# A static slot schedule for the backward pass of one-query attention, with the o sums taken over columns of E as weights

## The chip, the cores and the metric

The kernel runs on one core of a Trainium2 chip. The metric is the device time of one execution in microseconds. Each execution is classed as fast or slow, and only fast ones are compared.

The engines are called as the profile calls them. PSUM is the memory that PE's results go to in these kernels. Recorded texts and some headings say bank for the storage of one PSUM tile; the traces name tiles, and no run here shows banks. PE is TensorE's matmuls, PEld its weight loads. ACT is ScalarE, DVE is VectorE, POOL is GpSimd and SP issues the loads. PEclk is the granted TensorE clock: 1.0 is full speed.

## The reference

For 64 independent heads there is one query q, 8192 keys K and values V of 128 elements in bf16, and the gradient d of the output. The kernel returns the output o and the gradients dq, dK and dV.

```python
scores = einsum("bhqd,bhkd->bhqk", q, k) * scale      # Sq = 1, Sk = 8192, D = 128
p = softmax(scores)
o = einsum("bhqk,bhkd->bhqd", p, v)                   # and its vjp for grad_out
```

Per head this means s = K q, dp = V d, E = exp(scale (s - max)), the sums l = sum E and delta, then dS = E (dp - delta), dq = dS K, o = E V, and the outer products dK = dS q and dV = p d. K and V are read once and dK and dV written once: 8.39 MB per head, 537 MB in all.

## The kernel before

K and V come in with the keys on the partitions, so each 128x128 block is transposed on PE before it serves as weights for s and dp. A head has 8 chunks of 16 blocks, four of K and four of V.

```python
for w, src in enumerate((kt, vt)):
    for c in range(NCH):                                   # 4 chunks each
        tp = ps_tp.tile([P, CH, P], BF16, tag="tp")
        for i in range(CH):                                # 16 transposes, 128 columns moving
            nc.tensor.transpose(tp[:, i, :], src[:, c * CH + i, :], ident_bf[:])
        ev = evp.tile([P, CH, P], BF16, tag="ev")
        nc.scalar.copy(out=ev[:], in_=tp[:])               # eviction on ACT: out of PSUM
        for i in range(CH):                                # 16 score products, one column moving
            nc.tensor.matmul(sdp[:, w, n : n + 1], lhsT=ev[:, i, :], rhs=qdT[:, w, bh : bh + 1], ...)
# ... then the softmax chain: maximum (DVE, PE, DVE, PE, DVE), E_f (ACT), sums (PE), dS (DVE)
for w, (src, col, norm) in enumerate(((kt, dS_bf, rls), (vt, E_bf, rl))):
    for n in range(NT):                                    # 64 dq products, then 64 o products
        nc.tensor.matmul(acc[:, w : w + 1], lhsT=src[:, n, :], rhs=col[:, n : n + 1], ...)
# ... then 8 outer products of 1.22 us on DVE, and two stores
```

One PSUM tile per head, sdpw, holds s, dp, the transposed maximum, its broadcast and the two sums. The build orders the instructions by its own scheduler.

## Time and profile before

| | before |
|---|---|
| time, median of 9 runs | 1401.55 us (1393.88 to 1408.60) |
| PE, ACT, DVE busy | 88%, 71%, 53% |
| mean granted clock | 0.716 |
| first to last maximum of a head, 63 heads | 1342.7 us, 21.3 us per head |

The first view is the page of the kernel before: the busy times, two rows of the 40 slices (tenths of full clock, tenths of DMA time), and the chain of work that ended last, by engine.

```profile
PE 1228.4 (88%) x24964; PEld 1128.2 (81%) x24964; DVE 745.5 (53%) x1413; ACT 989.2 (71%) x769; POOL 69.2 (5%) x136
...
PEclk9776676777676766767777767667677777777675
DMA  8899999999999999999999999999999999999955
...
PE 43%; issue 32%; ACT 18%; DVE 4%; POOL 1%; DMA 1%; ACTq 0%; POOLq 0%
```

PE leads the chain with 43%, its clock is low for much of the time (0.716 in the mean), and DMA is nearly full all along (share 0.99 from 60 to 1330 us). The groups of instructions of the same page follow: line, engine, operation, output and inputs, shapes, count, then busy us and mean ns of one, then the idle time before them.

```profile
L115 PE MATMUL tp<-ident_bf,vt 128*128 128x128 bf16 x4096 | 450.2, 298 | 5.9 <-issue 5.9
...
L115 PE MATMUL tp<-ident_bf,kt 128*128 128x128 bf16 x4096 | 359.3, 229 | 3.4 <-issue 3.4
...
L214 PE MATMUL acc<-E_bf,vt 128*128 128x1 bf16 x4096 | 124.9, 166 | 35.5 <-issue 35.0
```

The same transposes are dearer for V than for K. The windows of the kernel before show why. Their columns are the stretch, its length, then busy us and count for PE, PEld, DVE, ACT and POOL, then granted clock, DMA share and GB/s.

```profile
714.30:717.70 3.40, 2.78 (x58) 2.36 (x56) 1.88 (x11) 2.99 (x5) 0.00 (x0) 1.00 1.03 434
717.70:721.10 3.40, 3.34 (x115) 3.22 (x113) 3.40 (x6) 1.49 (x2) 0.00 (x0) 0.94 0.95 405
721.10:724.50 3.40, 3.33 (x70) 3.06 (x67) 3.40 (x4) 1.95 (x2) 0.00 (x0) 0.50 1.02 414
724.50:727.90 3.40, 3.17 (x53) 3.11 (x54) 2.48 (x3) 2.57 (x3) 1.06 (x2) 0.50 1.15 422
727.90:731.30 3.40, 3.40 (x47) 3.15 (x44) 0.00 (x0) 3.11 (x2) 0.00 (x0) 0.55 0.87 347
731.30:734.70 3.40, 3.00 (x66) 2.62 (x65) 0.43 (x2) 3.30 (x2) 0.00 (x0) 1.00 1.00 429
```

The second window is almost all one-column dq and o products (115 matmuls). PE is busy for 3.34 of 3.40 us; the clock goes to 0.50 right after it and stays low for 10 us, in which V is transposed. The waits of the kernel before are the last view: who waited for whom, us in total, times, longest.

```profile
ACT ev L117 <- PE tp L115: 86.9, 157, 10.8
...
PE sdpw L120 <- ACT ev L117: 78.2, 207, 1.6
PE acc L214 <- issue: 35.2, 29, 2.4
```

PE waits some for the eviction that its scores need, and some for nothing that the profile shows. The full list has no wait of PE for a K or V load.

### The profile page before, as it was taken

Reading aid. Unit: us, or ns where it says so; the run is one execution under the profiler, and the core shown is the slowest. Engines: PE = TensorE matmul, PEld = TensorE weight load, DVE = VectorE, ACT = ScalarE, POOL = GpSimd, SP = SyncE. Lnnn points to the kernel's source line nnn. Section 1 sums busy time; section 2 is a strip of 40 time slices with the busy share of each in tenths; the row PEclk is TensorE's granted clock in tenths of the full one; section 3 lists DMA queues with packets and bytes.
Section 4 is the critical chain, followed back from the end, with each engine's and each line's share of the span. In section 5 each row is a group of like instructions: output and inputs, shape, how many; then the busy total and the mean of one; then the engine's idle time right before and its main releaser. Section 6 shows DMA issues by size and latency. Waiting matters only on the chain.

```text
span 1398.7 us, 53432 instructions
## 1 busy us (share of the span) xinstructions
PE 1228.4 (88%) x24964; PEld 1128.2 (81%) x24964; DVE 745.5 (53%) x1413; ACT 989.2 (71%) x769; POOL 69.2 (5%) x136
## 2 busy tenths in 40 slices
PE   5889899999889898899998988988888999888883
PEld 5888888888878788788888887888888888778883
DVE  1654645645645546456456546465464565464553
ACT  5667677777676676767777776767777777767672
POOL 0000000000000000000000000000000000000000
PEclk9776676777676766767777767667677777777675
DMA  8899999999999999999999999999999999999955
GB/s 362 356 378 392 380 389 384 415 407 415 398 401 373 396 377 392 403 376 413 407 408 414 398 394 397 394 375 397 377 395 406 412 410 414 412 377 406 373 240 242
DMA packets 37406, 540.37 MB, mean 386 GB/s; under 512 B 4416, under 2 KB 4416, under 8 KB 4416
## 3 DMA queue, kind: packets, MB, share of 16 engines
q1 hardware_dynamic: 18592, 268.48, 49.8%
q0 software_dynamic: 18432, 268.44, 45.3%
q8 instruction: 195, 3.19, 0.8%
q14 instruction: 27, 0.22, 0.0%
q10 hardware_dynamic: 160, 0.03, 0.0%
HBM read 268.47 MB, written 268.47 MB: 384 GB/s over the span
## 4 chain that ended last, share of the span: by engine, by line
PE 43%; issue 32%; ACT 18%; DVE 4%; POOL 1%; DMA 1%; ACTq 0%; POOLq 0%
PE tp L115 21%; ACT ev L117 17%; PE acc L214 12%; PE sdpw L120 8%; POOL out_dram L237 1%; DVE ob L228 1%; PE sdpw L136 1%; PE sdpw L165 1%; ACT oT L221 1%; DMA qd_nat<-in_grad_out_dram 1%; DVE dSu L182 1%; ACT E_f L143 1%; DVE negdelta L169 1%; DVE dS_bf L191 0%; PE sdpw L132 0%
## 5 line engine op out<-in xcount | busy, mean ns | idle before, releaser
L117 ACT COPY ev<-tp 128x2048 bf16<-128x2048 bf16 x512 | 934.5, 1869 | 90.1 <-PE tp L115 86.9
L115 PE MATMUL tp<-ident_bf,vt 128*128 128x128 bf16 x4096 | 450.2, 298 | 5.9 <-issue 5.9
L115 PEld LDWEIGHTS <-vt 128*128 128x128 bf16 x4096 | 397.3, 140 | 7.5 <-issue 7.5
L120 PEld LDWEIGHTS <-ev 128*128 128x128 bf16 x8192 | 265.0, 101 | 143.4 <-ACT ev L117 125.9
L120 PE MATMUL sdpw<-qdT,ev 128*128 128x1 bf16 x8192 | 293.6, 165 | 83.3 <-ACT ev L117 78.2
L115 PE MATMUL tp<-ident_bf,kt 128*128 128x128 bf16 x4096 | 359.3, 229 | 3.4 <-issue 3.4
L228 DVE TENSOR_TENSOR ob<-qb,Pn 128x2048 bf16<-128x2048 bf16 x256 | 306.7, 1219 | 0.2
L228 DVE TENSOR_TENSOR ob<-qb,dSs 128x2048 bf16<-128x2048 bf16 x256 | 296.1, 1220 | 0.0
L130 DVE TENSOR_REDUCE mp<-sdpw 128x1 f32<-128x64 f32 x64 | 14.4, 225 | 503.4 <-PE sdpw L120 503.4
L115 PEld LDWEIGHTS <-kt 128*128 128x128 bf16 x4096 | 262.1, 102 | 4.1 <-issue 2.3
L214 PE MATMUL acc<-E_bf,vt 128*128 128x1 bf16 x4096 | 124.9, 166 | 35.5 <-issue 35.0
L214 PEld LDWEIGHTS <-vt 128*128 128x128 bf16 x4096 | 121.0, 104 | 38.8 <-issue 38.8
L221 ACT ACTIVATE oT<-acc,rl 128x1 bf16<-128x1 f32 x64 | 16.9, 264 | 182.3 <-PE acc L214 182.3
L237 POOL DMA_DIRECT2D out_dram<-ob x128 | 68.2, 533 | 1318.2 <-DVE ob L228 1312.1
L214 PEld LDWEIGHTS <-kt 128*128 128x128 bf16 x4096 | 116.2, 100 | 12.8 <-issue 12.6
L214 PE MATMUL acc<-dS_bf,kt 128*128 128x1 bf16 x4096 | 115.6, 164 | 6.2 <-DVE dS_bf L191 3.0
L221 ACT ACTIVATE oT<-acc,rls 128x1 bf16<-128x1 f32 x64 | 16.9, 264 | 95.6 <-PE acc L214 95.6
L143 ACT ACTIVATE E_f<-sdpw,negm 128x64 f32<-128x64 f32 x64 | 20.1, 314 | 24.4 <-DVE negm L138 24.4
L165 PEld LDWEIGHTS sdpw<-ld,ones_f 128*128 128x128 f32 x128 | 19.2, 189 | 16.1 <-issue 14.9
L165 PE MATMUL sdpw<-ld,ones_f 128*128 128x2 f32 x128 | 22.8, 248 | 8.4 <-DVE ld L154 1.1
L134 DVE TENSOR_REDUCE gm<-sdpw 1x1 f32<-1x128 f32 x64 | 17.8, 278 | 23.4 <-PE sdpw L132 23.4
L106 DVE CAST qb<-qbp 128x256 bf16<-128x256 f32 x64 | 27.2, 424 | 5.8 <-PE qbp L98 3.7
(34 smaller groups left out, 249.9 us busy)
## 6 DMA issues: line engine op xcount, KB each, us to landing
out_dram<-ob POOLq DMA_DIRECT2D x128, 2048.0 KB, 16.0
kt<-in_k_dram SPq DMA_DIRECT2D x64, 2048.0 KB, 10.6
vt<-in_v_dram SPq DMA_DIRECT2D x64, 2048.0 KB, 17.0
out_dram<-on SPq DMA_DIRECT2D x2, 16.0 KB, 8.5
qd_nat<-in_q_dram ACTq DMA_DIRECT2D x1, 16.0 KB, 8.2
qd_nat<-in_grad_out_dram ACTq DMA_DIRECT2D x1, 16.0 KB, 10.2
```

The source lines that it names most:

```text
L106: nc.vector.tensor_copy(out=qb[:], in_=qbp[:])
L115: nc.tensor.transpose(tp[:, i, :], src[:, c * CH + i, :], ident_bf[:])
L117: nc.scalar.copy(out=ev[:], in_=tp[:])
L120: nc.tensor.matmul(sdp[:, w, n : n + 1], lhsT=ev[:, i, :], rhs=qdT[:, w, bh : bh + 1], start=True, stop=True,)
L130: nc.vector.reduce_max(out=mp[:], in_=sdp[:, 0, :], axis=AX.X)
L134: nc.vector.reduce_max(out=gm[:], in_=mT, axis=AX.X)
L143: nc.scalar.activation(out=E_f[:], in_=sdp[:, 0, :], func=ACT.Exp, bias=negm[:], scale=scale, accum_out=ld[:, 0:1],)
L165: nc.tensor.matmul(lsum, lhsT=ones_f[:], rhs=ld[:], start=True, stop=True)
L214: nc.tensor.matmul(acc[:, w : w + 1], lhsT=src[:, n, :], rhs=col[:, n : n + 1], start=(n == 0), stop=(n == NT - 1),)
L221: nc.scalar.activation(out=oT[:, w, bh : bh + 1], in_=acc[:, w : w + 1], func=ACT.Copy, scale=norm[:])
L228: nc.vector.tensor_tensor(out=ob[:, n0 : n0 + OC, :].rearrange("p n (e t) -> p n e t", t=2), in0=qb[:, w, :] .rearrange("p (e t) -> p e t" ...
L237: store_eng.dma_start(out=dst[bh], in_=ob[:])
```

## The change

The intent is to keep PE at an even load; that this would hold the full clock was my estimate. The work of a head is cut into eight slots. Slot s transposes chunk s of head i, takes a quarter of the o or dq sum of head i-1, and takes the scores of the chunk before. DVE makes one outer product per slot. Every computing instruction of the loop is pinned behind the one before it on its engine. The o sum turns round: a column of E (128x1) is the weight, and 128 columns of V move. The core of the diff follows. It is condensed: cuts are marked, some lines are joined.

```diff
+    pin = tc.keep_in_program_order
-    work = ctx.enter_context(tc.tile_pool(name="work", bufs=2))
+    work = ctx.enter_context(tc.tile_pool(name="work", bufs=3))
 ...
+    def begin(i):
+        h.sdpw = ps_sdp.tile([P, SDPW], F32, tag="sdp", name="sdpw")   # one tile, as before
+        h.s = h.sdpw[:, 0:NT]
+        h.dp = h.sdpw[:, NT : 2 * NT]
+        h.mT = h.sdpw[0:1, MT0 : MT0 + P]
+        h.mb = h.sdpw[:, MB0 : MB0 + 1]
+        h.lsum = h.sdpw[:, LS0 : LS0 + 2]
 ...
+    def acc_o(i, c):
+        for n in range(c * CH, (c + 1) * CH):
+            pin(nc.tensor.matmul(h.oacc[:], lhsT=h.E_bf[:, n : n + 1], rhs=h.vt[:, n, :], ...))
 ...
+    for g in range(SL * (BH + 2)):
+        i, s = divmod(g, SL)
 ...
+            ev = transpose_chunk(i, s)          # 16 transposes on PE, eviction on ACT
+        if live and s == 5: max_all(i)          # PE, then DVE (gm)
+        if live and s == 7: expo(i)             # ACT (E_f), then DVE (E_bf)
+        if one and s == 1:  normalise(i - 1)
+        if one:
+            if s < NCH: acc_o(i - 1, s)
+            else:       acc_dq(i - 1, s - NCH)
+        if live and s == 6: max_spread(i)       # PE, then DVE (negm)
+        if prev is not None: score_chunk(*prev) # 16 score products of the chunk before
+        if live and s == 4: max_part(i)         # DVE (mp)
 ...                                            # outer products: one per slot
```

Loads keep three buffers per tensor, stores two. K of the first head comes in four pieces.

More of the change, by code (lines that the diff above doesn't have):

```diff
@@ L15 @@
 CH = 16
-OC = 16
 @with_exitstack
@@ L39 @@
     NT = Sk // P
-    assert NT * P == Sk and NT % CH == 0
+    assert NT * P == Sk and NT == 4 * CH
     NCH = NT // CH
+    SL = 2 * NCH
     scale = float(D) ** -0.5
@@ L53 @@
     ps_sdp = ctx.enter_context(tc.tile_pool(name="ps_sdp", bufs=2, space=bass.MemoryType.PSUM))
-    ps_acc = ctx.enter_context(tc.tile_pool(name="ps_acc", bufs=1, space=bass.MemoryType.PSUM))
-    ps_qb = ctx.enter_context(tc.tile_pool(name="ps_qb", bufs=1, space=bass.MemoryType.PSUM))
+    ps_m = ctx.enter_context(tc.tile_pool(name="ps_m", bufs=2, space=bass.MemoryType.PSUM))
     qd_nat = const.tile([BH, 2, D], BF16)
-    nc.scalar.dma_start(out=qd_nat[:, 0, :], in_=q.rearrange("b h s d -> (b h s) d"))
-    nc.scalar.dma_start(out=qd_nat[:, 1, :], in_=grad_out.rearrange("b h s d -> (b h s) d"))
+    load_eng.dma_start(out=qd_nat[:, 0, :], in_=q.rearrange("b h s d -> (b h s) d"))
+    load_eng.dma_start(out=qd_nat[:, 1, :], in_=grad_out.rearrange("b h s d -> (b h s) d"))
     k_v = k.rearrange("b h (p n) d -> (b h) p n d", n=NT)
@@ L77 @@
     for w in range(2):
-        tps = ps_qb.tile([P, BH], BF16, tag="qb")
+        tps = ps_m.tile([P, BH], BF16, tag="m")
         nc.tensor.transpose(tps[:], qd_nat[:, w, :], ident_bf[:BH, :BH])
         nc.vector.tensor_copy(out=qdT[:, w, :], in_=tps[:])
-    oT = const.tile([P, 2, BH], BF16)
+    dqT = const.tile([P, BH], BF16)
+    o_all = const.tile([1, BH, D], BF16)
     MT0 = 2 * NT
@@ L88 @@
     SDPW = LS0 + 2
-    for bh in range(BH):
-        kt = kvp.tile([P, NT, D], BF16, tag="K")
-        load_eng.dma_start(out=kt[:], in_=k_v[bh])
-        vt = kvp.tile([P, NT, D], BF16, tag="V")
-        load_eng.dma_start(out=vt[:], in_=v_v[bh])
-        qbp = ps_qb.tile([P, 2, D], F32, tag="qb")
-        nc.tensor.matmul(
-            qbp[:],
-            lhsT=ident_bf[:BH, bh : bh + 1].to_broadcast([BH, P]),
-            rhs=qd_nat[:],
-            start=True,
-            stop=True,
-        )
-        qb = work.tile([P, 2, D], BF16, tag="qb")
-        nc.vector.tensor_copy(out=qb[:], in_=qbp[:])
-        sdpw = ps_sdp.tile([P, SDPW], F32, tag="sdp")
-        sdp = sdpw[:, 0 : 2 * NT].rearrange("p (a n) -> p a n", a=2)
-        for w, src in enumerate((kt, vt)):
-            for c in range(NCH):
-                tp = ps_tp.tile([P, CH, P], BF16, tag="tp")
-                for i in range(CH):
-                    nc.tensor.transpose(tp[:, i, :], src[:, c * CH + i, :], ident_bf[:])
-                ev = evp.tile([P, CH, P], BF16, tag="ev")
-                nc.scalar.copy(out=ev[:], in_=tp[:])
-                for i in range(CH):
-                    n = c * CH + i
-                    nc.tensor.matmul(
-                        sdp[:, w, n : n + 1],
-                        lhsT=ev[:, i, :],
-                        rhs=qdT[:, w, bh : bh + 1],
-                        start=True,
-                        stop=True,
-                    )
-        with tc.high_priority():
-            mp = work.tile([P, 1], F32, tag="mp")
-            nc.vector.reduce_max(out=mp[:], in_=sdp[:, 0, :], axis=AX.X)
-            mT = sdpw[0:1, MT0 : MT0 + P]
-            nc.tensor.transpose(mT, mp[:], ident_f[:])
-            gm = work.tile([1, 1], F32, tag="gm")
-            nc.vector.reduce_max(out=gm[:], in_=mT, axis=AX.X)
-            mb = sdpw[:, MB0 : MB0 + 1]
-            nc.tensor.matmul(mb, lhsT=ones_f[0:1, :], rhs=gm[:], start=True, stop=True)
-            negm = work.tile([P, 1], F32, tag="negm")
@@ new lines, with load_k, load_v @@
+    class Head:
+        pass
+    heads = [Head() for _ in range(BH)]
+    def load_k(i):
+        h = heads[i]
+        h.kt = kvp.tile([P, NT, D], BF16, tag="K", name="kt")
+        if i == 0:
+            for c in range(NCH):
+                load_eng.dma_start(
+                    out=h.kt[:, c * CH : (c + 1) * CH, :],
+                    in_=k_v[i, :, c * CH : (c + 1) * CH, :],
+                )
+        else:
+            load_eng.dma_start(out=h.kt[:], in_=k_v[i])
+    def load_v(i):
+        h = heads[i]
+        h.vt = kvp.tile([P, NT, D], BF16, tag="V", name="vt")
+        load_eng.dma_start(out=h.vt[:], in_=v_v[i])
@@ new lines, in broadcast @@
+    def broadcast(i):
+        h = heads[i]
+        qbp = ps_m.tile([P, 2, D], F32, tag="m", name="qbp")
+        pin(
+            nc.tensor.matmul(
+                qbp[:],
+                lhsT=ident_bf[:BH, i : i + 1].to_broadcast([BH, P]),
+                rhs=qd_nat[:],
+                start=True,
+                stop=True,
+            )
+        )
+        h.qb = work.tile([P, 2, D], BF16, tag="qb", name="qb")
+        pin(nc.vector.tensor_copy(out=h.qb[:], in_=qbp[:]))
+    def begin(i):
+        h = heads[i]
+        h.sdpw = ps_sdp.tile([P, SDPW], F32, tag="sdp", name="sdpw")
[4 more added lines that the diff above has]
+        h.lsum = h.sdpw[:, LS0 : LS0 + 2]
@@ new lines, in transpose_chunk, with score_chunk @@
+    def transpose_chunk(i, c):
+        h = heads[i]
+        src = h.kt if c < NCH else h.vt
+        n0 = (c % NCH) * CH
+        tp = ps_tp.tile([P, CH, P], BF16, tag="tp", name="tp")
+        for t in range(CH):
+            pin(nc.tensor.transpose(tp[:, t, :], src[:, n0 + t, :], ident_bf[:]))
+        ev = evp.tile([P, CH, P], BF16, tag="ev", name="ev")
+        pin(nc.scalar.copy(out=ev[:], in_=tp[:]))
+        return ev
+    def score_chunk(i, c, ev):
+        h = heads[i]
+        w = c // NCH
+        dst = h.s if w == 0 else h.dp
+        n0 = (c % NCH) * CH
+        for t in range(CH):
+            pin(
+                nc.tensor.matmul(
+                    dst[:, n0 + t : n0 + t + 1],
+                    lhsT=ev[:, t, :],
+                    rhs=qdT[:, w, i : i + 1],
+                    start=True,
+                    stop=True,
+                )
+            )
@@ new lines, in max_part, with max_all, max_spread @@
+    def max_part(i):
+        h = heads[i]
+        h.mp = work.tile([P, 1], F32, tag="mp", name="mp")
+        pin(nc.vector.reduce_max(out=h.mp[:], in_=h.s, axis=AX.X))
+    def max_all(i):
+        h = heads[i]
+        pin(nc.tensor.transpose(h.mT, h.mp[:], ident_f[:]))
+        h.gm = work.tile([1, 1], F32, tag="gm", name="gm")
+        pin(nc.vector.reduce_max(out=h.gm[:], in_=h.mT, axis=AX.X))
+    def max_spread(i):
+        h = heads[i]
+        pin(nc.tensor.matmul(h.mb, lhsT=ones_f[0:1, :], rhs=h.gm[:], start=True, stop=True))
+        h.negm = work.tile([P, 1], F32, tag="negm", name="negm")
+        pin(
@@ L138, with expo @@
             nc.vector.tensor_scalar(
-                out=negm[:], in0=mb, scalar1=-scale, scalar2=None, op0=ALU.mult
+                out=h.negm[:], in0=h.mb, scalar1=-scale, scalar2=None, op0=ALU.mult
             )
-            E_f = work.tile([P, NT], F32, tag="E_f")
-            ld = work.tile([P, 2], F32, tag="ld")
+        )
+    def expo(i):
+        h = heads[i]
+        h.E_f = work.tile([P, NT], F32, tag="E_f", name="E_f")
+        h.ld = work.tile([P, 2], F32, tag="ld", name="ld")
+        pin(
@@ L143 @@
             nc.scalar.activation(
-                out=E_f[:],
-                in_=sdp[:, 0, :],
+                out=h.E_f[:],
+                in_=h.s,
                 func=ACT.Exp,
-                bias=negm[:],
+                bias=h.negm[:],
                 scale=scale,
-                accum_out=ld[:, 0:1],
+                accum_out=h.ld[:, 0:1],
             )
-            E_bf = work.tile([P, NT], BF16, tag="E_bf")
-            nc.vector.tensor_copy(out=E_bf[:], in_=E_f[:])
-            junk = work.tile([P, NT], BF16, tag="junk")
+        )
@@ L154, with weigh @@
+        h.E_bf = work.tile([P, NT], BF16, tag="E_bf", name="E_bf")
+        pin(nc.vector.tensor_copy(out=h.E_bf[:], in_=h.E_f[:]))
+    def weigh(i):
+        h = heads[i]
+        junk = work.tile([P, NT], BF16, tag="junk", name="junk")
+        pin(
             nc.vector.tensor_tensor_reduce(
                 out=junk[:],
-                in0=E_f[:],
-                in1=sdp[:, 1, :],
+                in0=h.E_f[:],
+                in1=h.dp,
                 scale=1.0,
@@ L161, with normalise @@
                 op1=ALU.add,
-                accum_out=ld[:, 1:2],
+                accum_out=h.ld[:, 1:2],
             )
-            lsum = sdpw[:, LS0 : LS0 + 2]
-            nc.tensor.matmul(lsum, lhsT=ones_f[:], rhs=ld[:], start=True, stop=True)
-            rl = work.tile([P, 1], F32, tag="rl")
-            nc.vector.reciprocal(out=rl[:], in_=lsum[:, 0:1])
-            negdelta = work.tile([P, 1], F32, tag="negdelta")
+        )
+    def normalise(i):
+        h = heads[i]
+        pin(nc.tensor.matmul(h.lsum, lhsT=ones_f[:], rhs=h.ld[:], start=True, stop=True))
+        h.rl = work.tile([P, 1], F32, tag="rl", name="rl")
+        pin(nc.vector.reciprocal(out=h.rl[:], in_=h.lsum[:, 0:1]))
+        negdelta = work.tile([P, 1], F32, tag="negdelta", name="negdelta")
+        pin(
             nc.vector.tensor_scalar(
                 out=negdelta[:],
-                in0=lsum[:, 1:2],
-                scalar1=rl[:],
+                in0=h.lsum[:, 1:2],
+                scalar1=h.rl[:],
                 scalar2=-1.0,
@@ L176 @@
             )
-            rls = work.tile([P, 1], F32, tag="rls")
+        )
+        h.rls = work.tile([P, 1], F32, tag="rls", name="rls")
+        pin(
             nc.vector.tensor_scalar(
-                out=rls[:], in0=rl[:], scalar1=scale, scalar2=None, op0=ALU.mult
+                out=h.rls[:], in0=h.rl[:], scalar1=scale, scalar2=None, op0=ALU.mult
             )
-            dSu = work.tile([P, NT], F32, tag="dSu")
+        )
+        dSu = work.tile([P, NT], F32, tag="dSu", name="dSu")
+        pin(
             nc.vector.scalar_tensor_tensor(
                 out=dSu[:],
-                in0=sdp[:, 1, :],
+                in0=h.dp,
                 scalar=negdelta[:],
-                in1=E_f[:],
+                in1=h.E_f[:],
                 op0=ALU.add,
@@ L189 @@
             )
-            dS_bf = work.tile([P, NT], BF16, tag="dS_bf")
-            nc.vector.tensor_copy(out=dS_bf[:], in_=dSu[:])
-            Pn = work.tile([P, NT, 2], BF16, tag="Pn")
-            nc.vector.tensor_scalar(
-                out=Pn[:],
-                in0=E_f[:].unsqueeze(2).to_broadcast([P, NT, 2]),
-                scalar1=rl[:],
-                scalar2=None,
-                op0=ALU.mult,
-            )
-            dSs = work.tile([P, NT, 2], BF16, tag="dSs")
-            nc.vector.tensor_scalar(
-                out=dSs[:],
-                in0=dSu[:].unsqueeze(2).to_broadcast([P, NT, 2]),
-                scalar1=rls[:],
-                scalar2=None,
-                op0=ALU.mult,
-            )
-        acc = ps_acc.tile([P, 2], F32, tag="acc")
-        for w, (src, col, norm) in enumerate(((kt, dS_bf, rls), (vt, E_bf, rl))):
-            for n in range(NT):
+        )
+        h.dS_bf = work.tile([P, NT], BF16, tag="dS_bf", name="dS_bf")
+        pin(nc.vector.tensor_copy(out=h.dS_bf[:], in_=dSu[:]))
+        h.pair = []
+        for src, norm, tag in ((dSu, h.rls, "ds2"), (h.E_f, h.rl, "p2")):
+            d = work.tile([P, NT, 2], BF16, tag=tag, name="pair")
+            pin(
+                nc.vector.tensor_scalar(
+                    out=d[:],
+                    in0=src[:].unsqueeze(2).to_broadcast([P, NT, 2]),
+                    scalar1=norm[:],
+                    scalar2=None,
+                    op0=ALU.mult,
+                )
+            )
+            h.pair.append(d)
+    def acc_o(i, c):
+        h = heads[i]
+        if c == 0:
+            h.oacc = ps_m.tile([1, D], F32, tag="m", name="oacc")
+        for n in range(c * CH, (c + 1) * CH):
+            pin(
                 nc.tensor.matmul(
-                    acc[:, w : w + 1],
-                    lhsT=src[:, n, :],
-                    rhs=col[:, n : n + 1],
+                    h.oacc[:],
+                    lhsT=h.E_bf[:, n : n + 1],
+                    rhs=h.vt[:, n, :],
                     start=(n == 0),
@@ L220, with acc_dq, end_o @@
                 )
+            )
+    def acc_dq(i, c):
+        h = heads[i]
+        if c == 0:
+            h.qacc = ps_m.tile([P, 1], F32, tag="m", name="qacc")
+        for n in range(c * CH, (c + 1) * CH):
+            pin(
+                nc.tensor.matmul(
+                    h.qacc[:],
+                    lhsT=h.kt[:, n, :],
+                    rhs=h.dS_bf[:, n : n + 1],
+                    start=(n == 0),
+                    stop=(n == NT - 1),
+                )
+            )
+    def end_o(i):
+        h = heads[i]
+        pin(
@@ L221 @@
             nc.scalar.activation(
-                out=oT[:, w, bh : bh + 1], in_=acc[:, w : w + 1], func=ACT.Copy, scale=norm[:]
+                out=o_all[:, i, :], in_=h.oacc[:], func=ACT.Copy, scale=h.rl[0:1, :]
             )
-        for w, (dst, sc) in enumerate(((dk_v, dSs), (dv_v, Pn))):
-            ob = outp.tile([P, NT, D], BF16, tag=f"o{w}")
-            for n0 in range(0, NT, OC):
-                nc.vector.tensor_tensor(
-                    out=ob[:, n0 : n0 + OC, :].rearrange("p n (e t) -> p n e t", t=2),
-                    in0=qb[:, w, :]
-                    .rearrange("p (e t) -> p e t", t=2)
-                    .unsqueeze(1)
-                    .to_broadcast([P, OC, D // 2, 2]),
-                    in1=sc[:, n0 : n0 + OC, :].unsqueeze(2).to_broadcast([P, OC, D // 2, 2]),
-                    op=ALU.mult,
-                )
-            store_eng.dma_start(out=dst[bh], in_=ob[:])
@@ L239, with end_dq @@
-    for w, dst in enumerate((out_1, out_0)):
-        tps = ps_qb.tile([BH, P], BF16, tag="qb")
-        nc.tensor.transpose(tps[:], oT[:, w, :], ident_bf[:])
-        on = const.tile([BH, D], BF16, tag=f"on{w}")
-        nc.vector.tensor_copy(out=on[:], in_=tps[:])
-        load_eng.dma_start(out=dst.rearrange("b h s d -> (b h s) d"), in_=on[:])
+        )
+    def end_dq(i):
+        h = heads[i]
+        pin(
+            nc.scalar.activation(
+                out=dqT[:, i : i + 1], in_=h.qacc[:], func=ACT.Copy, scale=h.rls[:]
+            )
+        )
@@ new lines, in outer @@
+    def outer(i, w, c):
+        h = heads[i]
+        if c == 0:
+            h.ob = outp.tile([P, NT, D], BF16, tag=f"o{w}", name="ob")
+        n0 = c * CH
+        shape = [P, CH, D // 2, 2]
+        pin(
+            nc.vector.tensor_tensor(
+                out=h.ob[:, n0 : n0 + CH, :].rearrange("p n (e t) -> p n e t", t=2),
+                in0=h.qb[:, w, :]
+                .rearrange("p (e t) -> p e t", t=2)
+                .unsqueeze(1)
+                .to_broadcast(shape),
+                in1=h.pair[w][:, n0 : n0 + CH, :].unsqueeze(2).to_broadcast(shape),
+                op=ALU.mult,
+            )
+        )
+        if c == NCH - 1:
+            dst = dk_v if w == 0 else dv_v
+            store_eng.dma_start(out=dst[i], in_=h.ob[:])
@@ new lines @@
+    for j in range(min(2, BH)):
+        load_k(j)
+        load_v(j)
+    prev = None
+    for g in range(SL * (BH + 2)):
+        i, s = divmod(g, SL)
+        live = i < BH
+        one = 0 <= i - 1 < BH
+        two = 0 <= i - 2 < BH
+        if s == 0 and i + 1 < BH and i >= 1:
+            load_v(i + 1)
+            load_k(i + 1)
+        if live:
+            if s == 0:
+                begin(i)
+            if s == 1:
+                broadcast(i)
+            ev = transpose_chunk(i, s)
+        if live and s == 5:
+            max_all(i)
+        if live and s == 7:
+            expo(i)
+        if one and s == 1:
+            normalise(i - 1)
+        if one:
+            if s < NCH:
+                acc_o(i - 1, s)
+            else:
+                acc_dq(i - 1, s - NCH)
+        if live and s == 6:
+            max_spread(i)
+        if prev is not None:
+            score_chunk(*prev)
+        prev = (i, s, ev) if live else None
+        if live and s == 4:
+            max_part(i)
+        if one and s == 0:
+            weigh(i - 1)
+        if one and s == NCH - 1:
+            end_o(i - 1)
+        if one and s == SL - 1:
+            end_dq(i - 1)
+        if one and 2 <= s < 6:
+            outer(i - 1, 1, s - 2)
+        if one and s >= 6:
+            outer(i - 1, 0, s - 6)
+        if two and s < 2:
+            outer(i - 2, 0, s + 2)
@@ L248 @@
+    tps = ps_m.tile([BH, P], BF16, tag="m")
+    nc.tensor.transpose(tps[:], dqT[:], ident_bf[:])
+    dqn = const.tile([BH, D], BF16)
+    nc.vector.tensor_copy(out=dqn[:], in_=tps[:])
+    load_eng.dma_start(out=out_1.rearrange("b h s d -> (b h s) d"), in_=dqn[:])
+    load_eng.dma_start(out=out_0.rearrange("b h s d -> s (b h) d"), in_=o_all[:])
 _INS = ['q', 'k', 'v', 'grad_out']
```

## The prediction

> **What bounds it now.** In a steady stretch one head takes 20.4 us (timeline, 702 to 743 us). The view of who waited for whom lists no wait for a K or V load or for an output buffer; in the chain of waits PE and ACT alternate. PE sets the pace: per head 128 transposes, 128 one-column score products, 128 one-column dq/o products. V's transposes run at granted clock 0.5 (16 take 1.73 us), K's at 1.0 (0.9 us); the windows view shows the clock falling in the 3.5 us burst of one-column dq/o products and back some 10 us later. [...]the clock records here change in multiples of 3.41 us. Some heads add 1 to 3 us gaps of PE that nothing explains ("issue", 51 us in all); first and last maximum are 1342.7 us apart, 21.3 us per head.
>
> A second limit lies just behind: DMA. 537 MB at 384 GB/s; the packets fill 96% of the 16 engines' span, 1.00 in the 20 us windows with the 20.4 us period. A 16 KB packet takes at best 0.611 us, so 16 engines give 429 GB/s at most[...]. With both queues active the trace shows about 415; 20 us windows reach 416.
>
> **What the change does.**
> - It splits the burst: a slot has 16 transposes (128 columns moving), 16 o products (now 128 columns moving, one weight column) or 16 dq products, and 16 scores. [...]so I expect clock 1.0 most of the time.
> - Per head at full clock (estimates from traced costs): transposes 7.2 us (now 10.5), scores 3.6, dq 1.74, o 64 x 56 ns = 3.6 (now 1.74), small matmuls 1: 17 to 18 us of PE.
> - ACT 8 x 1.87 + 1 = 16 us, DVE about 12 us: below PE.
> - The softmax chain no longer stalls a stage.
> - DMA bytes unchanged; loads keep three buffers, stores two.
>
> **What lies on the critical path.** Compute drops from 21.3 to about 18 us per head, but 8.39 MB per head at 410 to 415 GB/s need 20.2 to 20.5 us. DMA becomes the limit and most of PE's gain is lost to waits for K or output buffers. Estimate: the middle 1270 us, at 394 GB/s now, shrink to 1270 x 394/412 = 1214; start (K of head 0 in chunks) and tail (shorter slots; DMA half idle in the last 60 us now) give some 8 us more: about 1335 us.[...] If PE fell to the low clock in each head: about 22 us per head, near 1400.
>
> **Prediction.** 1335 us, 1290 to 1385. Faster by over 2%: 0.83; within 2%: 0.13; slower: 0.04.
>
> **What would show it.** Mean granted clock from 0.72 to above 0.85. DMA share 1.00 and 405 GB/s or more in nearly all middle slices. V transposes: 16 in 0.9 us. New waits of PE for kt's DMA or of DVE for ob's store. ACT near 75 to 80% busy.
>
> **What would make it wrong.** [...]Waits for DMA may let the clock fall. Pinned order may make one late semaphore stall all engines. The DMA rate may depend on how loads and stores overlap.

The sum of the main forecast: 1214 us for the middle, 129 us for start and tail as they are now (1399 - 1270), less 8, is 1335 us. Beside it is a second case with a higher DMA rate, which came to 1295 us, near the lower end of the range. Clock 1.0 rests on one thing seen in the trace before: the clock falls in the burst of one-column products (1.00 from 719 to 720 us, 0.50 from 721 us). That the new slots would hold it was my estimate. The 429 GB/s is an estimate too: 16 engines, each with 16384 bytes in 0.611 us, the median of that trace's 32963 packets of this size (the shortest took 0.608 us). The busiest of its 20 us windows moved 424 GB/s.

## The result, and the profile after

| | before | after |
|---|---|---|
| time, median | 1399.66 us (4 runs) | 1501.99 us (1494.29 to 1511.83, 4 runs) |
| ratio of the fast runs | | 1.0725, 95% interval 1.0642 to 1.0807 |
| PE, ACT, DVE busy | 88%, 71%, 53% | 87%, 67%, 50% |
| mean granted clock | 0.716 | 0.824 |
| first to last maximum, per head | 21.3 us | 22.9 us (1441.5 / 63) |

A ratio is the mean time of one kernel's fast runs over that of the other's of the same rounds, so it is not quite the ratio of the medians quoted. Executions over 1.5% slower than the fastest of the same kernel are left out of the means. The kernel became 7% slower, outside the predicted range. The page of the changed kernel:

```profile
PE 1303.5 (87%) x24963; PEld 1211.7 (81%) x24963; DVE 747.4 (50%) x1412; ACT 995.7 (67%) x769; POOL 69.2 (5%) x136
...
PEclk9887887888878788788788887888788778888986
DMA  8898989999999999899899999999989989899966
...
PE 59%; issue 25%; ACT 7%; DVE 6%; POOL 1%; DMA 1%; SPq 0%; POOLq 0%; ACTq 0%
...
L144 PE MATMUL tp<-ident_bf,kt 128*128 128x128 bf16 x4096 | 342.2, 250 | 2.1 <-DMA kt<-in_k_dram 2.1
L276 PE MATMUL oacc<-vt,E_bf 128*1 128x128 bf16 x4096 | 332.4, 246 | 0.0
...
L144 PE MATMUL tp<-ident_bf,vt 128*128 128x128 bf16 x4096 | 295.3, 229 | 7.3 <-issue 5.3
```

PE still leads, with more of the chain. DMA did not become the limit (share 0.94): the middle (60 to 1270 us) ran at 367 GB/s, against 396 before. The low clock moved from V's transposes to K's, and the o product grew from 124.9 to 332.4 us. The waits of the changed kernel are new:

```profile
ACT ev L146 <- PE tp L144: 470.3, 443, 5.6
...
PE sdpw L156 <- ACT E_f L191: 121.6, 64, 2.3
...
PE sdpw L156 <- DVE negm L181: 16.0, 64, 0.3
PE sdpw L156 <- DVE gm L174: 15.1, 64, 0.4
```

In each of the 64 heads, score products of V wait for the exponential of s, for its maximum and for the broadcast of it. They need none of these: dp = V d has no part of s in it. The timeline of the changed kernel shows the longest of the waits in one head (start us, length, engine, line, what; in brackets the idle time before it and its releaser):

```profile
711.12 0.61 PE L292 MATMUL qacc<-dS_bf,kt 128*128 128x1 bf16 x16
711.42 1.86 ACT L146 COPY ev<-tp 128x2048 bf16<-128x2048 bf16 x1 [2.10 <-PE tp L144]
...
713.18 0.32 ACT L191 ACTIVATE E_f<-sdpw,negm 128x64 f32<-128x64 f32 x1
...
713.64 0.57 PE L156 MATMUL sdpw<-qdT,ev 128*128 128x1 bf16 x16 [1.91 <-ACT E_f L191]
```

The score products of chunk 6 write sdpw while E_f has yet to read it. E_f was traced before them (it comes first in the program), so they wait for it, and E_f stands on ACT behind the 1.86 us eviction of chunk 7. PE does nothing for 1.91 us, and being pinned it can do nothing else. The windows of the changed kernel around that wait:

```profile
706.20:709.60 3.40, 2.56 (x62) 2.46 (x60) 1.55 (x3) 2.88 (x2) 0.53 (x1) 0.95 1.05 395
709.60:713.00 3.40, 2.13 (x32) 2.07 (x31) 0.52 (x1) 1.58 (x1) 0.00 (x0) 0.50 0.95 328
713.00:716.40 3.40, 2.76 (x38) 2.56 (x38) 1.33 (x2) 1.11 (x5) 0.00 (x0) 0.50 0.97 410
716.40:719.80 3.40, 3.40 (x45) 2.94 (x43) 1.51 (x4) 1.50 (x1) 0.00 (x0) 0.54 1.05 448
719.80:723.20 3.40, 3.40 (x68) 3.16 (x66) 3.08 (x10) 2.38 (x2) 0.17 (x1) 1.00 0.55 227
```

The clock falls at the end of the first window, which holds the two shorter waits and a gap of 0.59 us that the profile does not explain. So the long wait for E_f did not start this low spell; it comes in it. The clock stays at 0.5 for 10 us, through slots 7, 0 and 1. In that spell 16 transposes take 1.73 instead of 0.92 us, and 16 o products 1.79 instead of 0.98 us, as the chain of work of the changed kernel shows (start us, us, what):

```profile
714.21 1.73 PE tp L144 x16
715.94 1.79 PE oacc L276 x16
...
721.67 0.92 PE tp L144 x16
722.59 0.98 PE oacc L276 x16
```

To compare kernels I divided PE's time in each trace by the start times of its matmuls. Of the time from one start to the next, up to 57 ns of a 128-column product, 45 ns of a one-column product and 280 ns of any other counts as its own work. For 128-column products what lies between 57 and 112 ns counts as low clock, and anything beyond 112 ns as idle; for all others everything beyond their own work counts as idle. The sizes are my choice, so the terms are rough. (In these two traces the median from one 128-column product to the next of its group was 55 to 56 ns at clock 1.0 and 107 ns at 0.5, and 25 and 27 ns for one-column products.) Us per head (total over 64):

| | transposes | scores | o | dq | other | low clock | idle | sum |
|---|---|---|---|---|---|---|---|---|
| before | 7.24 | 3.42 | 1.73 | 1.66 | 0.92 | 3.24 | 3.34 | 21.54 |
| after | 7.18 | 3.34 | 3.60 | 1.70 | 1.11 | 2.57 | 3.58 | 23.07 |

The change was to remove most of the last two terms. It took 0.67 us from the low clock, added 0.24 us to the idle time, and paid 1.87 us for the o product.

### The profile page after: what moved, and what is told of

It is laid out like the page before. It is cut to its first block, busy times and chain, and to the rows that moved or that the text cites. A ratio compares the mean times of both kernels' runs of the same rounds, so it can differ in the third digit from the quotient of the medians.

```text
span 1494.8 us, 53368 instructions
## 1 busy us (share of the span) xinstructions
PE 1303.5 (87%) x24963; PEld 1211.7 (81%) x24963; DVE 747.4 (50%) x1412; ACT 995.7 (67%) x769; POOL 69.2 (5%) x136
## 4 chain that ended last, share of the span: by engine, by line
PE 59%; issue 25%; ACT 7%; DVE 6%; POOL 1%; DMA 1%; SPq 0%; POOLq 0%; ACTq 0%
PE tp L144 26%; PE oacc L276 16%; PE sdpw L156 13%; ACT ev L146 6%; DVE ob L324 4%; PE qacc L292 2%; POOL out_dram L336 1%; PE sdpw L178 1%; ACT E_f L191 1%; PE qbp L118 1%; DMA vt<-in_v_dram 1%; DVE mp L168 1%; PE sdpw L221 1%; DVE gm L174 1%; DVE negm L181 1%
## 5 line engine op out<-in xcount | busy, mean ns | idle before, releaser
L324 DVE TENSOR_TENSOR ob<-qb,pair 128x2048 bf16<-128x2048 bf16 x512 | 611.6, 1216 | 0.0
L156 PE MATMUL sdpw<-qdT,ev 128*128 128x1 bf16 x8192 | 283.3, 164 | 154.6 <-ACT E_f L191 121.6
L276 PE MATMUL oacc<-vt,E_bf 128*1 128x128 bf16 x4096 | 332.4, 246 | 0.0
L144 PEld LDWEIGHTS <-kt 128*128 128x128 bf16 x4096 | 295.1, 114 | 14.5 <-issue 10.0
L144 PE MATMUL tp<-ident_bf,vt 128*128 128x128 bf16 x4096 | 295.3, 229 | 7.3 <-issue 5.3
L276 PEld LDWEIGHTS <-E_bf 128*1 128x1 bf16 x4096 | 277.5, 95 | 26.4 <-issue 12.2
L144 PEld LDWEIGHTS <-vt 128*128 128x128 bf16 x4096 | 251.6, 103 | 9.5 <-issue 7.5
L292 PE MATMUL qacc<-dS_bf,kt 128*128 128x1 bf16 x4096 | 142.2, 164 | 7.0 <-issue 7.0
L292 PEld LDWEIGHTS <-kt 128*128 128x128 bf16 x4096 | 136.0, 97 | 9.0 <-issue 8.3
L304 ACT ACTIVATE o_all<-oacc,rl 1x128 bf16<-1x128 f32 x64 | 22.6, 353 | 8.9 <-PE oacc L276 8.9
L178 PE MATMUL sdpw<-gm,ones_f 1*128 1x1 f32 x128 | 25.0, 261 | 0.9 <-issue 0.9
L118 PE MATMUL qbp<-qd_nat,ident_bf 64*128 64x256 bf16 x64 | 22.9, 358 | 0.0
```

The costliest lines, as they stand in the source:

```text
L118: nc.tensor.matmul(qbp[:], lhsT=ident_bf[:BH, i : i + 1].to_broadcast([BH, P]), rhs=qd_nat[:], start=True, stop=True,)
L144: pin(nc.tensor.transpose(tp[:, t, :], src[:, n0 + t, :], ident_bf[:]))
L156: nc.tensor.matmul(dst[:, n0 + t : n0 + t + 1], lhsT=ev[:, t, :], rhs=qdT[:, w, i : i + 1], start=True, stop=True,)
L178: pin(nc.tensor.matmul(h.mb, lhsT=ones_f[0:1, :], rhs=h.gm[:], start=True, stop=True))
L276: nc.tensor.matmul(h.oacc[:], lhsT=h.E_bf[:, n : n + 1], rhs=h.vt[:, n, :], start=(n == 0), stop=(n == NT - 1),)
L292: nc.tensor.matmul(h.qacc[:], lhsT=h.kt[:, n, :], rhs=h.dS_bf[:, n : n + 1], start=(n == 0), stop=(n == NT - 1),)
```

## The experiments

The theory (A): dp shares its tile with what ACT and DVE read, so PE's pinned products wait for the softmax chain, and the idle time helps to keep the clock low. Why products wait for reads of columns that they don't overlap is not shown here; what a run can show is whether the waits go when the tile is split. Rival (B): slots with one-column dq products keep the clock low, whatever the waits. Rival (C): o with one weight column costs too much.

### Two banks: e1_two_banks

```diff
-        h.sdpw = ps_sdp.tile([P, SDPW], F32, tag="sdp", name="sdpw")    # condensed: slices left out
+        h.sw = ps_sdp.tile([P, NT + P + 1], F32, tag="s", name="sw")     # s, mT, mb
+    def begin_v(i):                                                      # called in slot 4
+        h.dw = ps_sdp.tile([P, NT + 2], F32, tag="d", name="dw")         # dp, lsum
-    ps_sdp bufs=2
+    ps_sdp bufs=1                                                        # two tiles in all, as before
```

> The one tile in PSUM (scores s, dp, maximum, sums: one bank) is split into two tiles in two banks: s with the maximum, dp with the sums. Theory A (one bank for what PE writes and DVE/ACT read makes pinned PE wait, and the idle time then lets the clock fall): the score products' waits on E_f, negm and gm (153 us in all) fall under 15 us, mean granted clock rises from 0.82 to above 0.92, 1320 to 1370 us. Theory B (the slots with one-column dq products keep the clock down by themselves): waits gone, clock stays at 0.80 to 0.85, 1360 to 1400 us. Theory C (o with one weight column costs too much PE time): the waits were slack, time stays above 1450 us.

It took 1341.93 us (ratio to before 0.9589, interval 0.9548 to 0.9630), with clock 0.906. That is 160 us less than the changed kernel, by splitting one tile. The page and the waits of this run:

```profile
PEclk9998999898998888989889998899898899898886
DMA  9999999999999999999999999999999999999976
...
PE dw L160 <- issue: 21.6, 21, 2.0
PE tp L148 <- DMA kt<-in_k_dram: 18.9, 20, 2.9
```

No score product waits for E_f, negm or gm any more. Instead PE now waits for the load of K, and the DMA row is full: the middle ran at 411 GB/s. Theory A holds for the waits. The clock came out a little below what A expected (0.906 against 0.92).

### o as before: e2_v_weights

```diff
-                    lhsT=h.E_bf[:, n : n + 1],
-                    rhs=h.vt[:, n, :],
+                    lhsT=h.vt[:, n, :],
+                    rhs=h.E_bf[:, n : n + 1],
```

> Only the o product undone: V as weights, one column of E moving, as in the kernel before; one bank kept. PE saves about 2.2 us per head at full clock. Theory C: 1360 us or less. Theory A: waits stay near 150 us, and with fewer columns moving the clock falls (0.65 to 0.78), which gives part of the saving back: 1420 to 1500 us. Theory B: clock falls too, as A.

It took 1440.70 us (1.0295), with clock 0.669. The wait for E_f stayed at 120.6 us. Against the changed kernel PE saves 1.84 us of o per head (1.76 instead of 3.60) and loses 1.25 us to the low clock (3.82 instead of 2.57). So with the new form of o the clock is higher (0.824 against 0.669), as intended, but in this schedule it costs 61 us more than it brings. Rival C explains a part of the loss and not the whole: without the new o the kernel is still slower than before.

### Both: e3_banks_v_weights

> Two banks and V as weights for o. PE needs about 15.3 us per head at full clock, so DMA should bind if the clock holds: 1310 to 1350 us. If the columns of the o product are what keeps the clock up, the clock falls below that of the run with two banks alone (under 0.8) and the time is no better than it.

It took 1339.54 us (0.9565), with clock 0.719. The clock is as low as in the kernel before, and the time equals that of two banks alone. With DMA as the limit (411 GB/s from 100 to 1200 us), neither the o form nor the clock (0.719 against 0.906) shows in the time.

### The exponential ahead of the last eviction: e5_exp_first

```diff
+            if s == 7:
+                expo(i)
             ev = transpose_chunk(i, s)
```

> One bank kept; the exponential is traced before the eviction of the last chunk, so that it no longer stands behind 1.87 us of copy on ACT. Theory A: the wait for E_f (121 us) falls under 45 us, the waits for negm and gm (31 us) stay, the clock rises some; 1400 to 1450 us. Theory B and C: at most 2% faster, clock unchanged.

It took 1348.42 us (0.9643), better than theory A expected, with one tile kept and clock 0.868. The waits of this run no longer have E_f as a releaser of PE; the other two are unchanged:

```profile
PE sdpw L156 <- DVE negm L181: 15.9, 64, 0.3
PE sdpw L156 <- DVE gm L174: 15.0, 64, 0.4
```

Per head the idle time went from 3.58 to 1.80 us and the low clock from 2.57 to 2.06 us. So the wait for E_f is most of the loss, and it takes two things together: the shared tile, and E_f's place behind 1.86 us of copying on ACT. Moving either away is enough to get below the kernel before.

### No pinning: e4_unpinned

```diff
-    pin = tc.keep_in_program_order
+    pin = lambda ins: ins
```

> The changed kernel with one bank, but its instructions not pinned: the build's scheduler may reorder them as in the kernel before. If the pinned order is needed for the waits on the shared bank, the scheduler moves other work ahead of them: waits of score products on E_f, negm and gm below 80 us, 1350 to 1450 us. If the bank alone makes the waits, whatever the order: within 2% of 1502 us.

It took 1362.83 us (0.9728), with clock 0.891. The score products' waits for E_f, negm and gm were 2.8 us in all. Free to reorder, the build put other work ahead of them: its timeline has K's transposes of the next head in that place. So the pinned order is the third condition of the loss, as far as one run that frees the whole order can show it.

### Filling the waits: e6_filled

```diff
+        if live and s in FILL:                     # FILL = {5: 4, 6: 16, 7: 28}
+            junk_ps = ps_m.tile([P, P], F32, tag="m", name="fill")
+            for _ in range(FILL[s]):
+                pin(nc.tensor.matmul(junk_ps[:], lhsT=ident_bf[:], rhs=ident_bf[:], ...))
```

> The changed kernel, one bank and its waits kept, with 4, 16 and 28 extra products of 128 moving columns (2.7 us per head at full clock, results not used) put in front of the three waiting score chunks. If idle time lets the clock fall and the low clock costs some 3 us per head: clock above 0.92 and 1380 to 1480 us, faster in spite of more work. If the low clock has another cause: clock at most 0.85, slower than 1502 us.

It took 1481.20 us (1.0581), with clock 0.951: 20 us faster than the changed kernel with 2.69 us more of PE work in each head, and 1 us over the expected range. Low clock fell from 2.57 to 1.22 us per head and idle time from 3.58 to 2.13 us. The filling takes up the waiting time (no wait for gm is left, and 11.7 us for E_f). With moving columns in place of idle time the clock was 0.951 instead of 0.824. It is a demonstration, not a cure: the filling costs what it brings.

### One part alone, in the kernel before: e7_before_e_weights

> The kernel before, with one part of the change alone: o with columns of E as weights, 128 columns of V moving. If moving columns keep the clock: clock from 0.72 to above 0.82, V's transposes near 0.9 us per 16, and the longer o product (1.7 to 3.6 us) about paid for: 1330 to 1400 us. If a weight of one column doesn't count: clock 0.70 or less, o product 6.8 us, above 1500 us.

The edit puts columns of E as weights and V as the moving side into the old kernel. It took 1529.69 us (1.0916), with clock 0.843, so neither theory's time and clock came together. The timeline shows the o products of two heads:

```profile
715.02 5.15 PE L225 MATMUL acc<-vt,E_bf 128*1 128x128 bf16 x64
...
739.59 6.46 PE L225 MATMUL acc<-vt,E_bf 128*1 128x128 bf16 x64
```

The clock had fallen at about 711 us, just before the first dq burst, and at about 738 us, at the end of the second, and was back after about 718 and 745 us. So these 64 o products ran for a large part in the low spell and took 5.2 and 6.5 us instead of 1.7 (over all heads 341.8 us, 5.3 us in the mean). After that the clock was up for part of V's transposes. The mean clock rose from 0.72 to 0.84 and the time rose by 9%: the low clock's cost per head hardly moved (3.24 to 3.13 us), and the o product's own work doubled (1.73 to 3.64 us).

### Is DMA the limit of the two-bank kernel? e8_banks_half_store and e9_after_half_store

```diff
-            store_eng.dma_start(out=dst[i], in_=h.ob[:])
+            store_eng.dma_start(out=dst[i, :, 0 : NT // 2, :], in_=h.ob[:, 0 : NT // 2, :])
```

Half of dK and dV is not written, so the results are wrong; o and dq stayed right.

> Two banks, and only half of each dK and dV tile stored (wrong results on purpose): 25% less DMA traffic, all computing kept. If DMA binds the two-bank kernel at 1342 us: DMA share falls well below 1 and the time to 1150 to 1210 us, the pace of PE (17.5 to 18.5 us per head). If PE binds it: above 1300 us.

> The changed kernel, one bank, half of each dK and dV tile stored (wrong results on purpose). If its loss is compute waiting for itself and not DMA, nothing is gained: 1470 to 1510 us, against 1269 us for the two-bank kernel with half stores. If DMA contention made the loss: below 1420 us.

With two tiles the time fell from 1342 to 1259.09 us, in the one fast run; the other run, 1278.54 us, is slow. (The 1269 us of the expectations below and above is the median of the two.) With all stores (e1) DMA's share was 1.00 in the middle, and PE waited for the load of K 20 times (18.9 us); with half stores the share is 0.95 and 0.93 in the two heads below, and PE waits for K once (2.1 us). The kernel was bound by DMA, but PE's own pace is nearer than I had estimated: the expected 1150 to 1210 us was too low. With one tile the time fell from 1502 only to 1463.16 us (2 runs), a little under the expected 1470: DMA contention made at most 39 us of it. Windows of the two-tile run, two whole heads:

```profile
704.20:722.50 18.30, 17.45 (x394) 16.28 (x391) 11.60 (x22) 15.27 (x13) 1.06 (x2) 1.00 0.95 353
722.50:740.90 18.40, 17.55 (x400) 16.50 (x398) 11.59 (x22) 15.52 (x13) 1.06 (x2) 1.00 0.93 346
```

These heads take 18.3 to 18.4 us at clock 1.0 throughout, the dq slots included, and the mean of the run is 0.950. That rules out rival B as it was put: in these heads such slots don't lower the clock by themselves. It is also the 18 us per head that the prediction gave for the changed kernel, but with the waits gone.

### The two forms of o without DMA's limit: e12_v_weights_half_store

> Two banks, V as weights for o, half of each tile stored (wrong results on purpose), to compare the two forms of o where DMA does not bind; with E as weights this took 1269 us. The V form saves 1.9 us of PE per head at full clock and loses what the low clock takes. If the columns of the o product pay for themselves: clock under 0.8 and 1260 us or more. If not: 1150 to 1240 us.

It took 1277.60 us (2 runs, 1269.19 and 1286.00), with clock 0.776, against 1259.09 us and clock 0.950 in the one fast run of the E form. So the V form, with 1.9 us less work of PE per head, was not faster: the first reading. Whether the E form is better by 1 or 2% or the two are worth the same, three runs don't decide.

### Both fixes, and a better end: e10_banks_exp_first and e13_store_halves

> Two banks and the exponential ahead of the last eviction. Less waiting of PE than either fix alone (1342 and 1348 us). If DMA is the common floor: 1330 to 1345 us, DMA share 1.0, waits of PE for K's load at least as large as with two banks alone (19 us). If waits of PE still set the time: below 1320 us.

Two tiles with the exponential first took 1339.27 us (0.9561). Two cures together bring no more than one: DMA is the common floor (410 GB/s in the middle, DMA share 1.00, and 20.7 us of PE waiting for K).

```diff
-        if c == NCH - 1:
-            store_eng.dma_start(out=dst[i], in_=h.ob[:])
+        if c % 2 == 1:
+            m0 = (c - 1) * CH
+            store_eng.dma_start(out=dst[i, :, m0 : m0 + 2 * CH, :], in_=h.ob[:, m0 : m0 + 2 * CH, :])
```

> Two banks, exponential first, and each dK and dV tile stored in two halves as soon as two of its four chunks are there (right results). Stores start 2.4 us earlier, which shortens the end and evens out DMA: 1320 to 1342 us; if DMA's rate in the middle is all that counts, within 5 us of the run without halves.

Storing each tile in two halves took 1335.73 us (5 runs; 0.9526, interval 0.9496 to 0.9555), with right results. It is the lowest median, 4.7% below the kernel before, though it is also within 5 us of the run without halves, so that both readings fit. Its waits show the floor plainly, for now DVE waits for its output buffers:

```profile
DVE ob L328 <- DMA out_dram<-ob: 179.1, 63, 6.1
```

## Why the prediction was wrong

- **What bounds the kernel before: right.** PE paces it, with the clock low for V's transposes; the runs that freed PE from the waits were all faster than before. The low clock alone is not the bound: with two tiles and V as weights (e3) the clock was 0.719, as before, and the time 1340 us.
- **DMA just behind, near 412 GB/s: right, and shown.** Every kernel with PE freed from waits and all its stores stopped at 1336 to 1342 us with 410 to 411 GB/s in the middle. The predicted 1335 us is within 1% of 1342 us, the time of the change without its flaw.
- **"The softmax chain no longer stalls a stage": wrong, and this is the step that failed.** I had read that the parts of the chain lie a slot apart, and concluded that nothing waits. I had not asked which other instructions touch the same PSUM tile. In the kernel before, the scores of V were traced ahead of the chain, so no score product waited for the chain there. In the slots they come between its parts. PE's products of V waited 153 us (121.6 + 16.0 + 15.1) for reads of columns they don't touch. With dp in a tile of its own these waits and 160 us of time were gone; with only the wait for E_f gone, 154 us were.
- **"So I expect clock 1.0 most of the time": wrong in this kernel.** The mean rose only to 0.82, below the 0.85 that I had named as the sign. The low spells moved to slots 7, 0 and 1, where PE now had 128-column o products as well as transposes, so the cost fell by only 0.67 us per head while the mean clock rose by 0.11. With the waits away and DMA relieved (e8), the two heads shown ran at 1.0 throughout and the mean was 0.950, as predicted.
- **Compute "about 18 us per head": wrong for this kernel.** It was 22.9 us. The work at full clock was well estimated: 16.9 us by the division of PE's time (17 to 18 predicted). The missing 6.15 us are 3.58 idle and 2.57 low clock.
- **o for 3.6 us instead of 1.74: right** (3.60 and 1.73). I had taken for granted that the clock would pay for it. In the changed kernel it did not (61 us slower than with V as weights). Without the waits it cost nothing that shows at DMA's limit (1342 against 1340 us).
- **What would make it wrong: named but underweighted.** "Pinned order may make one late semaphore stall all engines" and "Waits for DMA may let the clock fall" are close to what came. I gave slower 0.04. One more fear was groundless: that PE would stay at 0.5 with products of one weight column. In the same schedule the clock was 0.824 with them and 0.669 without them.

How far does the low clock follow from the waits? Idle time and low clock fell together with filling (3.58 to 2.13 and 2.57 to 1.22 us per head) and with the exponential first (3.58 to 1.80 and 2.57 to 2.06). A count says more. The clock records of the traces before and after change in multiples of 3.41 us. Both traces were cut into pieces on that grid, and the products with 128 or more moving columns that start in each piece were counted (the very ends left out): 836 pieces. After a piece with 20 or fewer the clock was at 0.5 in all 304 cases; after a piece with 26 or more it was at 1.0 in all 362. After the 170 pieces with 21 to 25 both occurred (1.0 in 90). PE's busy time separates the pieces far worse: its best threshold is right for 78% of them, that of the count for 95%. This is a count over two traces, and why the clock goes with it is not shown.

From it I estimate that in these kernels a slot whose only such products are 16 transposes keeps the clock up if it passes in about 2.1 us (16/26 of 3.41 us). The dq slots of the half-store run took 1.7 to 2.1 us from one group of transposes to the next (700 to 723 us), at clock 1.0. In the head of the changed kernel shown above, slots 6 and 7 took 3.2 and 4.6 us, waits included, and the clock was at 0.5 from the end of slot 6. So the waits may go with the low clock because they stretch the slots, and this is left of rival B: by this estimate the dq slots have little margin.

## What to carry to other kernels

Before pinning an order, list for each PSUM tile every engine that reads or writes it, and give a tile of its own to whatever is written while another engine's chain still reads; here products waited 153 us for data that they don't use. Put a short instruction that many wait for ahead of the long copy on the same pinned engine: here one line moved was worth 154 us. And judge a change of the clock by the work that runs while it is low, not by its mean: twice here the mean clock rose (0.716 to 0.824, and to 0.843 in e7) and the time rose too (by 7% and 9%).
